# Attention and gated FFN on one core: scores and P V as separate TensorE operations, strided P V in eight array tiles and four PSUM banks, under a new order

## The chip, the cores and the metric

The kernel runs on one core of a Trainium2 chip. The metric is device time in microseconds, from one launch to its end, taken as the median of a few runs. One further run was taken by the hardware profiler; all rows below come from it.

## What is computed

Attention over 8 batches and 8 heads with 576 positions and a head size of 64, then a gated feed-forward network over the 4608 tokens. Half of the heads see the last 32 positions (local), the other half see every 32nd earlier position (strided):

```python
scores = scale * np.matmul(q, k.transpose(0, 1, 3, 2))
rel = pos[:, None] - pos[None, :]
mask_local = (rel >= 0) & (rel < stride)                      # stride = 32, heads 0..3
mask_strided = (rel >= 0) & (pos[None, :] % stride == pos[:, None] % stride)   # heads 4..7
attn = softmax(np.where(masks, scores, -1e9))
x = np.matmul(attn, v)            # regrouped to (4608, 512)
xn = x / rms(x) * rms_g           # then, 512 -> 1536 -> 512:
out = (silu(xn @ w_gate) * (xn @ w_val)) @ w_out
```

## The kernel before

**Two kinds of TensorE work.** The feed-forward part is a long row of large products with a 128x128 weight and 512 columns (lines L579, L655, L1043, L1208, L1431, L1632 of the profile, "GEMM" below). Each takes one weight load and one matmul on the engine. The attention part is many small fp32 products, which take two weight loads and two matmuls each. In the trace one such product is therefore two records of each kind.

**Attention is done in 32 items**, eight batches times four pairs of heads; in each batch the order of pairs is local, strided, local, strided (KCO). For one item there are two bursts of small products and a softmax between them:

- `scores`: local, L290, 36 products (72 records), 64x32 weights against 64 columns; strided, L296, 64 products (128 records), 64x18 weights against 18 columns. They write `pair_`, a PSUM tile of two banks. The strided ones use two row halves of the array and, in each, two of the four 32-column groups: four tiles, all into the first bank.
- `soft`: DVE scales and masks out of `pair_` into a SBUF tile (L324; pp0, pp1, pT0, pT1 by turns), takes the row maximum (L326); ACT does the exponentials, for the odd items with DVE or GpSimd; then a reciprocal, a product and a 32x32 transpose (L344).
- `values` (P V): local, L307, 44 products (88 records), from four row groups into two column halves, eight tiles, in `pair_` and `acc01` (two banks each); strided, L313, 64 products (128 records), from four row groups, each into one column half: four tiles, in the two banks of `acc01`. For items 4 to 7 `acc01` is in use elsewhere and all of P V goes to `pair_`; the local ones are then done in two halves.
- `evac`: ACT or DVE copies the result to `raw` (L378, L380).

**Operations and the order.** Every step is recorded as an operation in `Plan`: an engine, what it reads and writes, and a function that issues all of its instructions in a row. `visit(s, v)` records the scores of item s and the P V of item v; where both are given, they are ONE TensorE operation, so that nothing can stand between them. An operation of strided scores and local P V has 64 + 44 products, one of local scores and strided P V 36 + 64. `Plan.order` then issues the operations in a sequence that the text `ORDER` gives: it is decoded to an index and an engine for each step (some operations may go to one of two or three engines). Within an engine the sequence is that of the program; between engines semaphores hold it. `evac` also reads a key "sv", which `soft` writes: the copies of item v come after the scaling of item s.

**Where the visits lie.** The first five items come at the start, before the FFN has input. Visits then stand beside the GEMMs of the first chunks of 512 tokens, the last of them about 800 us into the span.

Of the kernel before, what the change touches and what calls it, by code (L numbers as in the profile page):

```python
# [23 lines left out]
STRIDE = 32  # L24
NROW = S // STRIDE
P = 128
# [34 lines left out]
    "c-rk*S!^W7d9M1ax~lJcx_j=E91b}om&@g`%O#iGU25+`T4}XfuB6p{!8&3~mSjnmZ3&VsCsve1vaVb(VkEKyBys!@1j%y(1Of7thrH!EK!6x|PIXoHa1G=&Kpt2#=;^"  # L61
    "7h`s+Ww|NH+TgV+lR(mcz4$_z9yY(|I~nBM*7yZXIGg<Dr6i<`cAnZCl#I*ji=%FlA|p=VDLcCXF1?j}^bre89y9@Wp=`UQHCM!UvcoN?b{I}4lR$F|1*wL512?QN~@j"
    "lDUx@*f*BbolR^^H-10td15hSPR+%CS9lcz4P>6NBr<SIW%&nmxljz$lZ1D=m=Q0Gi5IfeqoO-yXn}&fnEE{p56Pi#h>>UetN87uV;t89NK?fokBnUi>&|o$3Gwa-d9<"
    "#{?RYHi@*5rueyFM`{AEgKlrj){bHr@-jAz)_{lQK{%H2g&wqdL*%$3kKbvWP+G~G8I<4RN=%dfR7=Au{|I_N4`SI`maP{Ml8iVYk6aC-((H1d3B$W@|uaMUJt#{s;ef"
    "hgTc=?0uweP?8+Iw%ki{s&KtpbBL>0Z?PZSv~M2iObW`C9nyZ-lGgZoIJahX2&-55~8@cPqa5=FP9)u6`#z|IN2r!5jCd(Q8TcQqXwe`Nr4cllAzS6Y;ZWnwz(t+<Y`V"
    "^~n6g4?p$H!`Tz?#L;x^kw<2arw>K9AB-Mbug~F|H)=O3)$8}wtJmgkUAQ}3xH5Zo{)LOx*4%Sf<Ezc5Mo(TEUCiRObMfk#q<1Sh-F@Ixa(!dxTH0<`Z{B}JUus<&E#G"
    "~2E4wk%x-@rjA!{Y+`R(K%&L-)p&C}JL-S*$_m?v0s)7c~&Q5+pxKN_vA{cP>4uTG>}tDDhEbS%k^CQ-7wn2jn+=`dZKo*z__sFw|g>zypi*1wyrCFxt~a{8^qY4UOU&"
    "2jqjT=wB?_FLHpdoRAQm!=Oy@3fNU+o)0b=Qr!-w`#A~YOltPR~qp*>Swds-(`(Bs6Cfd<CE1ah?B;8Tu<ZYs<moT%fe<FC3i>dt6_Z@*2A#b2^**5@N!hCU5MiF`21a"
    "Nf=*4J9Cemv{NeGof2=iFZ|$yiTER+dx!vlwvSzTB;#!jVHGk1x@aKDDf9{w+yF1$%Me*{sA1qCUgCh$e^{8hr`G?}gcws6T$Nh>sGv#$Wx9|4Oy4~)gxbMvQTUEcYvE"
    "kcO>)f@Yt`|DCbvT$0JUbiN>CjFrJGQJ&5)RsxD2y6mGt}zQVqj*wnV<T}wpH;qy_3f+-|B54({*Q$Hb?9AnZ*^unKlg@W^{cHJ0WM5+iTam?Rwi~&D69jrnQ|~TZzR?"  # L70
    "7P%o433`|<F(+f`b#Ce02-%h3#^uY?%K;yp<7fNa<ELHb?DSgAovkLbs}_4L>zLJSWieUEhRHNDc>g7~8nPqP?C@>Y>a<v^$!5iShK+}FR~Ff&1;)na-1(tCUFq^ZYj+"
    "8w4YE+*T3tO(HfrSP^5Q>|g(b2)PsYRlB-3Py%n>%4BEv4FgEk>&n=Pl=Aiayd?d@KDt4qGDk?OBVW~Ik|MP`%H(tN_n^iqtVKQlfu^NuzgeEV(E@BS2iG9Gk)0{uULU"
    "c1}syy(JutI<ICZ*X&|`L}C_YSoo09yhah8hed}>`$`!S~ge1z3L_0!1eREcP5D|anekW(aL6JZDYu?Z~%Cx;uFZcjguScC|Gx^(=Ylsb;1DoN1j1p!?XM$TA%jN^1$u"
    "eo`amugQ#gYr|mv!7?#yEs$LBxx_&}OQ!!dOiu7fDbzNU<FT488xM^#{8Lc+0O=-kg-PUYur6CHyNLDI_>w+G@5T<*xa1*>fSogr$dh7BkH4M7r;ikKQogJR=wPOMIr&"
    "m4B9H`9)4$#JOgBlctLu@e}v=-?ydio_-3myH*OvjJo$19OR)^6j~isidT;<|{1<8PQ~{@*l~oHIrhj-L4!6b;O92L-JFwTK6GhSJw@CCliX8U7Lv!>Iswr-NyI0DsC|"
    "C*ZiT$5Im+`i8FYKw|=IhfW<HGrq_w+=zf_@prU-#HPS`z3-2G1TGp^oLPvBuw{fsYeukm-EK4;%d@~tjih2=oreL}EbP<3b`8sMES6BZVHk|lCZi71EG8ThhOXg1ZP+"
    "e%sLd>cKltQ>bhJmU7NdhqyGCikVwOgX1uQ<j>x1v~!Lv8FH<8mKCaIbR(WzdKI7ah0o%0e5(G1w&bgZ7`02l+%fkOrm6Q*4XG(zLxG9m;#(>5J249_(Iagm062_M3Yb"
    "82fE<@!`8Zo91GvQBJLy;-a2h@>fj>lA@`k8wBXSFY=q0b?6ulMsdpK4Xzhyb1cohPHW(13e0`N5Fje#xlBf%QWu2apPWo{W`vnqif96G(;J?z>$s4v<W)R`AH6lY3R5"
    "{j~_Qz=?c@AO^VP<9Idb;Li}4ez!(P8X!P7|zz_A%t*JeXTKfIBo*?MioA)6LJ&N!##Mf6jI)|3EBZp6urOF{hA`T;O#v|g$Hf$JJt6P8*q^}YbE?rv2QEw5?>-ai9#r"
    "r#s+q!(E6=AC#te^VUR?x2sBN3#KG+0~%8X<TL`Mx$ndW+igjW%teUJq5TpeshR)<N2(%HeHjWHz->Y>rUJ^IQ>_&~?J*K)=us(hS^xV+!*D>2|v<Cu-x61^9Ul2boTM"  # L80
# [1856 lines left out]
```

## Time and profile before

| | |
|---|---|
| median of 3 runs | 1015.37 us (1014.62 to 1020.02) |
| the profiled execution | 1013.67 us |
| its span, first to last instruction | 1011.9 us |
| TensorE busy (matmul) | 949.3 us, 94% |
| VectorE busy | 747.2 us, 74% |
| ScalarE busy | 429.3 us, 42% |
| GpSimd busy | 231.9 us, 23% |
| mean granted TensorE clock | 0.96 |

TensorE is the engine to read. Its 10,244 matmuls are pipelined and their ends are modelled, so the start of one record against the start of the next tells more than the busy time. An idle time that a row ascribes to "issue" is one for which the profile shows no semaphore that was waited for.

### The profile page before, as it was taken

Reading aid. Unit: us, or ns where it says so; the run is one execution under the profiler, and the core shown is the slowest. Engines: PE = TensorE matmul, PEld = TensorE weight load, DVE = VectorE, ACT = ScalarE, POOL = GpSimd, SP = SyncE. Lnnn points to the kernel's source line nnn. Section 1 sums busy time; section 2 is a strip of 40 time slices with the busy share of each in tenths; the row PEclk is TensorE's granted clock in tenths of the full one; section 3 lists DMA queues with packets and bytes.
Section 4 is the critical chain, followed back from the end, with each engine's and each line's share of the span. In section 5 each row is a group of like instructions: output and inputs, shape, how many; then the busy total and the mean of one; then the engine's idle time right before and its main releaser. Section 6 shows DMA issues by size and latency. Waiting matters only on the chain.

```text
span 1011.9 us, 24518 instructions
## 1 busy us (share of the span) xinstructions
PE 949.3 (94%) x10244; PEld 772.5 (76%) x10244; DVE 747.2 (74%) x1247; ACT 429.3 (42%) x1006; POOL 231.9 (23%) x198
## 2 busy tenths in 40 slices
PE   4799998999989899999899999999998999999998
PEld 2687876778868787778677878887777788888887
DVE  4779987878757889978467888745486898446884
ACT  5678755233224447333443544442233634233240
POOL 2131233024223411122212322200001140003521
PEclk9689999999999999999989999999898999999999
DMA  9736666676564777838645569873354587765552
GB/s 347 307 142 223 215 221 213 236 282 255 166 229 148 249 249 228 307 149 298 248 157 191 188 202 316 303 277 126 125 202 134 165 282 266 275 243 203 177 163 107
DMA packets 95102, 222.97 MB, mean 220 GB/s; under 512 B 9616, under 2 KB 28688, under 8 KB 94992
## 3 DMA queue, kind: packets, MB, share of 16 engines
q1 hardware_dynamic: 94560, 220.85, 62.8%
q8 instruction: 80, 1.31, 0.5%
q10 hardware_dynamic: 432, 0.56, 0.2%
q14 instruction: 30, 0.25, 0.1%
HBM read 174.19 MB, written 47.19 MB: 219 GB/s over the span
## 4 chain that ended last, share of the span: by engine, by line
PE 58%; DMA 3%; DVE 2%; issue 2%; SPq 1%; POOL 0%; ACT 0%; POOLq 0%; DVEq 0%
PE acc L1632 10%; PE g L1632 7%; PE v L1632 7%; PE acc L1431 6%; PE v L1431 4%; PE g L1431 4%; PE g L1043 3%; PE acc L1043 3%; PE v L1043 3%; PE pair L1043 2%; PE g L1208 2%; PE acc L1208 2%; PE v L1208 2%; PE acc L313 2%; DMA xl<-to 1%
## 5 line engine op out<-in xcount | busy, mean ns | idle before, releaser
L579 PE MATMUL g<-xh,wg 128*128 128x512 f32 x184 | 60.1, 409 | 3.5 <-DVE e L594 3.5
L579 PE MATMUL v<-xh,wv 128*128 128x512 f32 x184 | 60.4, 410 | 0.1
L579 PEld LDWEIGHTS g<-xh,wg 128*128 128x128 f32 x184 | 34.7, 195 | 11.7 <-DVE e L594 4.7
L579 PEld LDWEIGHTS v<-xh,wv 128*128 128x128 f32 x184 | 35.5, 197 | 8.2 <-ACT or L1795 0.5
L710 POOL TENSOR_TENSOR tt<-tt 128x256 f32<-128x256 f32 (+1 forms) x29 | 25.1, 872 | 68.4 <-DVE tt L710 25.1
L579 PE MATMUL v<-xl,wv 128*128 128x512 f32 x92 | 37.3, 405 | 0.0
L579 PE MATMUL g<-xl,wg 128*128 128x512 f32 x92 | 36.8, 400 | 0.0
L579 PE MATMUL acc<-xh,wv 128*128 128x512 f32 x104 | 35.6, 426 | 1.1 <-DVE wg L623 1.1
L579 PE MATMUL acc<-xh,wg 128*128 128x512 f32 x104 | 33.8, 407 | 0.0
L1632 PE MATMUL acc<-wg,wv 128*128 128x512 f32 x102 | 31.1, 416 | 0.2 <-DMA wv<-wsv 0.2
L330 ACT ACTIVATE pT<-pT,mx 128x64 f32<-128x64 f32 x80 | 26.7, 335 | 10.2 <-DVE mx L326 10.2
L1632 PE MATMUL acc<-wv,wv 128*128 128x512 f32 x102 | 30.6, 410 | 0.0
L592 ACT ACTIVATE e<-g 128x512 f32<-128x512 f32 x23 | 13.7, 597 | 39.4 <-PE g L579 32.6
L1650 ACT ACTIVATE or<-g 128x512 f32<-128x512 f32 x24 | 14.4, 599 | 37.7 <-PE g L1632 37.4
L342 POOL TENSOR_TENSOR pp<-pp,mx 128x288 f32<-128x288 f32 (+1 forms) x7 | 6.7, 963 | 101.8 <-DVE mx L340 92.9
L655 PE MATMUL acc<-or,hh 128*128 128x512 f32 x96 | 30.1, 394 | 0.0
L296 PEld LDWEIGHTS pair<-xx,xx 64*18 64x18 f32 x2048 | 18.3, 94 | 12.9 <-issue 8.3
L330 ACT ACTIVATE pp<-pp,mx 128x64 f32<-128x64 f32 x80 | 26.7, 339 | 2.7 <-DVE mx L326 2.7
L296 PE MATMUL pair<-xx,xx 64*18 64x18 f32 x2048 | 20.1, 181 | 7.4 <-issue 4.0
L378 ACT COPY raw<-acc 128x256 f32<-128x256 f32 (+7 forms) x41 | 19.0, 538 | 18.1 <-PE acc L313 18.1
L324 DVE SCALAR_TENSOR_TENSOR pT<-pair,cb 128x640 f32<-128x640 f32 (+1 forms) x16 | 10.2, 638 | 21.9 <-PE pair L307 10.8
L579 PEld LDWEIGHTS acc<-xh,wv 128*128 128x128 f32 x104 | 21.4, 208 | 6.3 <-DVE wg L623 1.5
(878 smaller groups left out, 2982.4 us busy)
## 6 DMA issues: line engine op xcount, KB each, us to landing
wv<-wsv SPq DMA_DIRECT2D x36, 512.0 KB, 7.0
wg<-wsg SPq DMA_DIRECT2D x26, 512.0 KB, 7.2
or<-tg SPq DMA_DIRECT2D x22, 512.0 KB, 5.7
th<-tg SPq DMA_DIRECT2D x21, 512.0 KB, 5.6
tl<-tg SPq DMA_DIRECT2D x21, 512.0 KB, 5.7
xx<-in_qT_dram SPq DMA_DIRECT2D x32, 288.0 KB, 5.7
xx<-in_kT_dram SPq DMA_DIRECT2D x31, 288.0 KB, 5.4
vt<-in_vs_dram SPq DMA_DIRECT2D x16, 512.0 KB, 7.2
```

The source lines that it names most:

```text
L296: nc.tensor.matmul(out=pair_[32 * y:32 * y + NROW, 0, NROW * g:NROW * g + NROW], lhsT=q[r, z:z + NROW], rhs=k[r, z:z + NROW], start=True, ...
L313: nc.tensor.matmul(out=dst[0][64 * (y // 2):64 * (y // 2) + 64, y % 2, c], lhsT=v[k, j], rhs=t[k, 32 * j:32 * j + NROW], start=True, stop= ...
L330: nc.scalar.activation(out=tv[:, g], in_=tv[:, g], func=AF.Exp, bias=m[:, g:g + 1], accum_out=z[:, g:g + 1])
L378: nc.scalar.copy(out=d, in_=s)
L579: nc.tensor.matmul(out=out, lhsT=wt[:, w, sl], rhs=xhl[x, kc], start=(n == 0 and i == 0), stop=(n == KC - 1 and i == 2))
L655: nc.tensor.matmul(out=acc[t], lhsT=x[h][:, sl], rhs=wt[:, w], start=(u == 0 and i == 0), stop=(u == NU - 1 and i == 2))
L710: elementwise(width, lambda e: both(e).tensor_tensor(out=dst(), in0=a(), in1=b(), op=ALU.subtract), [], keys)
L1043: nc.tensor.matmul(out=banks[bk], lhsT=w, rhs=X[a, k].tile(y), start=start and k == 0 and i == 0, stop=stop and k == 1 and i == 2, skip_gr ...
L1208: nc.tensor.matmul(out=banks[bks[j]], lhsT=tile(v, k, j), rhs=x.tile(y), start=start and k == 0 and i == 0, stop=stop and k == KT - 1 and ...
L1431: nc.tensor.matmul(out=banks[bks[j]], lhsT=w.tile(v, k, j), rhs=x.tile(k, y), start=start and n == 0 and i == 0, stop=stop and n == KT - 1 ...
L1632: nc.tensor.matmul(out=banks[bk], lhsT=w, rhs=xtile(a, k, y), start=start and k == 0 and i == 0, stop=stop and k == 1 and i == 2, skip_gro ...
L1650: op("ACT", act(CH, True), 0, lambda: nc.scalar.activation(out=temp(dst), in_=banks[bk], func=AF.Copy, scale=scale), reads=bank_keys(bk), ...
```

## The change

- `visit` records the scores and the P V as two operations, each with its own place in the order. The largest has 64 small products. The scores of item s stand ahead of the P V of item v in the list.
- Strided P V: for each of eight j, four row groups times two column halves are issued, so eight tiles follow each other, and each row group has its own PSUM bank, two in `pair_` and two in `acc01`. Items 6 and 7 are done in two halves in `pair_`. The host lays V out to suit (`vs`).
- Strided scores: two row halves times four column groups, eight tiles, into both banks of `pair_`, 18 columns in every 64. Scaling reads them there (`flat`).
- The first memset clears all of `pair_` (1024 columns, before 128).
- `evac` of a strided item copies two pieces per chunk of 512 tokens instead of one, and no longer reads "sv".
- `ORDER` is another text. The number of matmuls of every line is the same.

```diff
-    op("DVE", 200, -1, lambda: nc.vector.memset(pair_[:, :, 256:320], 0.0), writes=PRK)
+    op("DVE", 1100, -1, lambda: nc.vector.memset(flat, 0.0), writes=PRK)
...
-        for g in range(16):
-            for y in range(4):
-                r, z = slice(64 * (y // 2), 64 * (y // 2) + 64), PAD + NROW * (16 * (y % 2) + g)
-                nc.tensor.matmul(out=pair_[32 * y:32 * y + NROW, 0, NROW * g:NROW * g + NROW], lhsT=q[r, z:z + NROW], rhs=k[r, z:z + NROW],
-                                 start=True, stop=True)
+        for j in range(8):
+            for z, y in enumerate(QZ):
+                for h in range(2):
+                    r, a = slice(64 * h, 64 * h + 64), PAD + NROW * (8 * z + j)
+                    nc.tensor.matmul(out=pair_[32 * y:32 * y + NROW, h, 64 * j:64 * j + NROW], lhsT=q[r, a:a + NROW], rhs=k[r, a:a + NROW],
+                                     start=True, stop=True)
...
-        for j in range(16):
-            for y in range(4):
-                k, c = slice(32 * y, 32 * y + NROW), slice(NROW * j, NROW * j + NROW)
-                nc.tensor.matmul(out=dst[0][64 * (y // 2):64 * (y // 2) + 64, y % 2, c], lhsT=v[k, j], rhs=t[k, 32 * j:32 * j + NROW],
-                                 start=True, stop=True)
+        for j in range(8):
+            for z in zs[1:] + zs[:1]:
+                r, c = slice(32 * QZ[z], 32 * QZ[z] + NROW), 320 + NROW * j
+                for h in range(2):
+                    g = 8 * h + j
+                    nc.tensor.matmul(out=dst[z // 2][64 * h:64 * h + 64, z % 2, c:c + NROW], lhsT=v[r, g], rhs=t[r, 32 * g:32 * g + NROW],
+                                     start=True, stop=True)
...
-            pair_[:, 0, 0:G * w].rearrange("q (g k) -> q g k", k=w), tv, mstr)
+            flat.rearrange("q (g k) -> q g k", k=64)[:, :, 0:w], tv, mstr)
...
-                moves.append((o.rearrange("p (i s n) -> p s n i", s=2, n=16),
-                              dst[0][:, :, 0:288].rearrange("p s (n i) -> p s n i", i=NROW)[:, :, :, i0:i1]))
+                    moves.append((o.rearrange("p (i s n) -> p s n i", s=4, n=8)[:, z:z + 2],
+                                  src[:, :, 320:320 + 8 * NROW].rearrange("p s (n i) -> p s n i", i=NROW)[:, :, :, i0:i1]))
...
-        op("ACT", act(t1 - t0, True) + 97 * (len(moves) - 1), 0, fn, reads=keys + ["sv"], writes=[("raw", c % NX, p) for c in cs],
+        op("ACT", act(t1 - t0, True) + 97 * (len(moves) - 1), 0, fn, reads=keys, writes=[("raw", c % NX, p) for c in cs],
...
-            op("PE", cost, 0, lambda fns=tuple(fns): [f() for f in fns], reads=reads + [("tb", v % 4), ("vt", v % 2)],
-               writes=writes + [k for k in keys if k not in writes])
...
+        if s is not None:
+            op("PE", 970 if its[s][1] < 2 else 1070, 0, lambda: scores(s), reads=[("xx", slot_of(s, 0)), ("xx", slot_of(s, 1)), ("xp", slot_of(s, 1))],
+               writes=PRK)
...
+            for dst, zs, keys in ([((pair_, pair_), (0, 1), PRK), ((pair_, pair_), (2, 3), PRK)] if 4 <= v < 8 else
+                                  [((pair_, acc01), (0, 1, 2, 3), PRK + A01K)]):
+                op("PE", (1250 if local else 1150) - 50 * (4 <= v < 8), 0, lambda dst=dst, zs=zs: values(v, dst, zs),
+                   reads=[("tb", v % 4), ("vt", v % 2)], writes=keys)
```

On TensorE, before, at the eighth strided scores of the program (about 293 us into the span). L579 is the FFN's first product; L296 the strided scores, L307 the local P V of the item before; a count behind a row is of products.

```order
L579 MATMUL v<-xh_874,wv_719 128x512 x2
L579 MATMUL v<-xl_883,wv_719 128x512
L296 MATMUL pair<-xx_80,xx_83 18x18 x64
L307 MATMUL pair<-pT_97,vt_85 64x32 x2
L307 MATMUL acc_69<-pT_97,vt_85 64x32 x4
L307 MATMUL pair<-pT_97,vt_85 64x32 x2
L307 MATMUL pair<-pT_97,vt_85 64x64 x2
L307 MATMUL acc_69<-pT_97,vt_85 64x64 x4
```

On TensorE, now, at the same scores (L298 is the old L296, L564 the old L579).

```order
L564 MATMUL acc_71<-xh_897,wv_721 128x512 x2
L564 MATMUL acc_71<-xl_900,wv_721 128x512
L298 MATMUL pair<-xx_80,xx_83 18x18 x64
L564 MATMUL acc_70<-xh_536,wg_1146 128x512 x2
L564 MATMUL acc_70<-xl_538,wg_1146 128x512
L564 MATMUL acc_70<-xh_665,wg_1146 128x512 x2
L564 MATMUL acc_70<-xl_714,wg_1146 128x512
L564 MATMUL g<-xh_897,wg_929 128x512 x2
```

Before, the 108 small products stood in one piece; now 36 GEMM products stand between the scores and the same local P V.

On TensorE, before, at the local scores and the strided P V that come next (L290 and L313).

```order
L579 MATMUL acc_70<-xl_883,wg_903 128x512
L290 MATMUL pair<-xx_82,xx_81 32x64 x36
L313 MATMUL acc_69<-pT_98,vt_86 64x18 x64
L579 MATMUL g<-xh_606,wg_987 128x512 x2
L579 MATMUL g<-xl_616,wg_987 128x512
```

On TensorE, now, the end of a local P V and the start of a strided P V in the middle of the attention (L309 is the old L307, L317 the old L313, L1416 the old L1431).

```order
L309 MATMUL pair<-pT_97,vt_85 64x64 x2
L309 MATMUL pair<-pT_97,vt_85 64x32 x4
L1416 MATMUL acc_71<-wv_3744,or_4227 128x512 x3
L1416 MATMUL acc_71<-wg_3966,wg_3928 128x512 x3
L317 MATMUL pair<-pT_98,vt_86 64x18 x2
L317 MATMUL acc_69<-pT_98,vt_86 64x18 x4
L317 MATMUL pair<-pT_98,vt_86 64x18 x4
```

The strided P V now alternates between `pair` and `acc`, and so needs what the local P V left in both to be copied out; here six GEMM products stand between the two.

## Rows read from the trace of the kernel before

**Rows 1.** The page: busy us of each engine; granted clock in 40 slices, tenths.

```profile
PE 949.3 (94%) x10244; PEld 772.5 (76%) x10244; DVE 747.2 (74%) x1247; ACT 429.3 (42%) x1006; POOL 231.9 (23%) x198
...
PEclk9689999999999999999989999999898999999999
```

**Rows 2.** TensorE's waits, 60 to 812 us: total us, times, longest.

```profile
PE acc L307 <- issue: 7.6, 4, 2.0
PE pair L307 <- issue: 6.2, 2, 4.0
PE acc L313 <- issue: 4.6, 3, 3.9
PE g L1632 <- issue: 4.4, 2, 3.7
...
PE acc L1632 <- issue: 3.1, 1, 3.1
PE pair L290 <- issue: 1.6, 1, 1.6
```

**Rows 3.** DMA queues, whole span, then 295.2 to 299.7 us: packets, MB, share.

```profile
q8 instruction: 80, 1.31, 0.5%
...
q8 instruction: 1, 0.02, 1.3%
```

**Rows 4.** Timeline of TensorE around 296 us: start, length, what, idle before.

```profile
293.78 1.23 PE L296 MATMUL pair<-xx,xx 64*18 64x18 f32 x128
...
299.66 0.38 PE L307 MATMUL pair<-pT,vt 32*64 32x64 f32 x3 [3.99 <-issue]
...
301.57 0.63 PE L579 MATMUL acc<-xl,wv 128*128 128x512 f32 x1
...
302.85 0.63 PE L579 MATMUL acc<-xl,wv 128*128 128x512 f32 x1
```

**Rows 5.** Stages: length, busy us of each engine, granted clock, DMA share, GB/s.

```profile
152.58:156.00 3.42, 3.42 (x16) 2.73 (x9) 0.69 (x1) 2.90 (x4) 0.00 (x0) 0.50 0.50 164
...
790.88:794.29 3.41, 3.41 (x10) 2.66 (x9) 3.38 (x8) 3.27 (x9) 0.00 (x0) 0.50 0.95 253
sum 51.21, PE 47.08 PEld 37.28 DVE 27.89 ACT 14.62 POOL 5.25; mean PE 4.28 PEld 3.39 DVE 2.54 ACT 1.33 POOL 0.48
```

**Rows 6.** Timeline of TensorE, small products without a stall, full clock.

```profile
87.29 0.90 PE L307 MATMUL pair<-pp,vt 32*64 32x32 f32 x48
...
100.19 0.39 PE L579 MATMUL g<-xl,wg 128*128 128x512 f32 x1
...
100.87 0.39 PE L579 MATMUL g<-xl,wg 128*128 128x512 f32 x1
101.19 1.23 PE L296 MATMUL pair<-xx,xx 64*18 64x18 f32 x128
102.34 0.50 PE L655 MATMUL acc<-or,hh 128*128 128x512 f32 x1
...
253.21 0.24 PE L307 MATMUL pair<-pp,vt 32*64 32x32 f32 x2
...
254.07 0.32 PE L307 MATMUL pair<-pp,vt 32*64 32x64 f32 x8
```

**Rows 7.** The same view: local scores and strided P V in one operation.

```profile
390.02 0.97 PE L290 MATMUL pair<-xx,xx 64*32 64x64 f32 x72
390.92 2.06 PE L313 MATMUL acc<-pT,vt 18*64 18x18 f32 x128
392.90 0.50 PE L1431 MATMUL acc<-wv,xl 128*128 128x512 f32 x1
```

**Rows 8.** The copies of P V on ACT: shortest, median, longest in ns.

```profile
L378 ACT COPY raw<-acc x41: 220/405/1150, 32.7 to 806.0; 128x256 f32<-128x256 f32 x14, 128x64 f32<-128x64 f32 x10, 128x128 f32<-128x128 f32 x5, 128x512 f32<-128x512 f32 x4
```

**Rows 9.** Stages as in Rows 5: the attention beside the first chunks.

```profile
60.00:353.00 293.00, 275.79 (x3713) 224.09 (x3712) 237.21 (x401) 139.43 (x349) 88.88 (x78) 0.97 0.63 218
353.00:418.00 65.00, 63.50 (x853) 51.20 (x852) 58.10 (x99) 34.02 (x90) 11.71 (x9) 1.00 0.75 245
```

More of the change, by code (lines that the diff above doesn't have):

```diff
@@ L65 @@
[L65 to L80, printed above, removed]
@@ L104 @@
+    "Pg6xfc2!Krx2vG4WFtdHAf*;2)%(>;z`G_$M3Rn=r&NipmYb5r$;wArD=LZq&G?G$>ymfLipcuRDe!O0eT|J8&(0CBKevv<@^H*U;th2#pDTlld}}J)AKPXZuS0rpZl4"
+    "+qDCzs$K3p1zyAdzrr2)"
 )
@@ L324, in soft @@
         op("DVE", dve(G * w), 0, lambda: nc.vector.scalar_tensor_tensor(out=ov, in0=sv, scalar=0.125, in1=mk, op0=ALU.mult, op1=ALU.add),
-           reads=["cb"] + PRK, writes=[tk, "sv"])
+           reads=["cb"] + PRK, writes=[tk])
         op("DVE", dve(G * w), 0, lambda: nc.vector.tensor_reduce(out=m, in_=tv, axis=AX.X, op=ALU.max, negate=True), reads=[tk], writes=[mk_])
@@ L355, in evac @@
             cs.append(c)
[L356 to L372 removed]
+            for z in zs[::2]:
+                src, o = dst[z // 2], raw[c % NX][:, p, max(0, lo - CH * c):hi - CH * c]
+                if p > 1:
+                    i0, i1 = (lo - base) // STRIDE, (hi - base) // STRIDE
+                    moves.append((o.rearrange("p (i s n) -> p s n i", s=4, n=8)[:, z:z + 2],
+                                  src[:, :, 320:320 + 8 * NROW].rearrange("p s (n i) -> p s n i", i=NROW)[:, :, :, i0:i1]))
+                    continue
+                m = 32 * (QB[z + 1] - QB[z])
+                a, e = max(lo - base, 32 * QB[z]) - 32 * QB[z], min(hi - base, 32 * QB[z + 2]) - 32 * QB[z]
+                at = base + 32 * QB[z] - CH * c
+                if a == 0 and e == 2 * m:
+                    moves.append((raw[c % NX][:, p, at:at + e].rearrange("p (z q) -> p z q", z=2), src[:, :, 320:320 + m]))
+                    continue
+                for f in range(2):
+                    a1, e1 = max(a, m * f), min(e, m * f + m)
+                    if a1 < e1:
+                        moves.append((raw[c % NX][:, p, at + a1:at + e1], src[:, f, 320 + a1 - m * f:320 + e1 - m * f]))
             lo = hi
@@ L416, in visit @@
                 load(s + 2)
-        else:
+        if v is not None:
+            local = its[v][1] < 2
+            for dst, zs, keys in ([((pair_, pair_), (0, 1), PRK), ((pair_, pair_), (2, 3), PRK)] if 4 <= v < 8 else
+                                  [((pair_, acc01), (0, 1, 2, 3), PRK + A01K)]):
+                op("PE", (1250 if local else 1150) - 50 * (4 <= v < 8), 0, lambda dst=dst, zs=zs: values(v, dst, zs),
+                   reads=[("tb", v % 4), ("vt", v % 2)], writes=keys)
+                evac(v, dst, zs, keys)
             done_i.add(v)
```

116 lines of the change are left out of this document (45 added, 71 removed).

## The prediction

> **What bounds the kernel now.** I read the page first: TensorE is busy for 949.3 of 1011.9 us and no other engine passes 74% [rows 1]. So its 62.6 us without work, and whatever makes its work slow, decide. Next I read what ended its idle times. Between 60 and 812 us, where the visits lie beside the GEMMs, the six largest waits on "issue" make 7.6 + 6.2 + 4.6 + 4.4 + 3.1 + 1.6 = 27.5 us [rows 2]; no wait on another engine is among them. Then one of these places, in order of time: strided scores run from 293.78 us, the local P V behind them is cut off, and TensorE stands still for 3.99 us before 299.66 [rows 4]. In that gap the queue of kind "instruction" carries one packet [rows 3].
>
> That row tells what "issue" is. Over the span this queue carries 80 packets, 1.31 MB, so 16.4 KB each [rows 3]. TensorE has 10,244 matmul and 10,244 weight-load records [rows 1]; 20,488 / 80 = 256 per packet. So each packet brings 256 TensorE instructions. GEMM products use two of them per 0.227 us (three products from 100.19 to 100.87 us [rows 6]), a block lasts 29 us, and the next packet has long landed. Small products use two per 8 to 15 ns, and a block is over in 1 to 2 us, before the next has come. An operation with 108 products is 432 instructions and is sure to hold most of a block.
>
> A second loss hangs on the first. The granted clock falls to 0.5 in eleven stretches after 60 us, 51.2 us in all [rows 5], which is 1.2 GHz instead of 2.4. Ten of them begin within some 2 us of a stop of at least 1 us in TensorE's stream; the one of rows 4 is among them. In it three GEMM products take from 301.57 to 302.85 us, 0.427 us each against 0.227.
>
> **The change part by part.** All sums go against the profiled execution, 1013.7 us; the median of the runs, 1015.4, is 1.7 above it.
>
> *Array tiles for strided P V.* 128 records take 2.06 us; less the 0.2 us that a lone record takes (two take 0.24 [rows 6]) and over 127 steps that is 14.6 ns a record [rows 7]. Is this the number of tiles? The local P V in halves, which uses four tiles too, takes (0.90 - 0.2) / 47 = 14.9 ns [rows 6]; the same product in eight tiles goes from 253.21 to the end of its last record at 254.39, (1.18 - 0.2) / 87 = 11.3 ns [rows 6]. So the tiles count. One end is 11.3: same weights, same tiles, but more columns. The other is the 8.1 ns of strided scores, (1.23 - 0.2) / 127 [rows 6]: same 18 columns, narrower weights. I take the middle, 9.7: 127 x 4.9 ns = 0.62 us for each of the 14 items that get eight tiles (items 6 and 7 keep four), **8.7 us less**; ends 5.9 and 11.6.
>
> The Trainium skill speaks against this term: "TensorE: Matmul & The Clock Gate", section "Wait — 56ns, not 53.3ns?", says that start to start never drops below about 25 ns however few the columns, so that tiles would bring nothing here and the sum would be 8.7 us higher. The traced records start 8 to 15 ns apart, so the trace doesn't agree, and the sum goes by the rows.
>
> *Strided scores in eight tiles.* Nothing here has their shape. I keep 8.1 ns; bounds are half of it (8 us less over 16 items of 127 steps), and the 10.8 ns of local scores in eight tiles, (0.97 - 0.2) / 71 [rows 7] (5.5 us more).
>
> *More operations.* 24 bursts stand alone that were parts of one (22 fused visits, two halves). The switch from GEMM to small product costs 101.19 - 100.87 = 0.32 us against 0.227 of a plain step [rows 6], so **2.2 us more**; at most 0.2 each, 5 us.
>
> *Instruction packets.* I cut the order of before and the new one into blocks of 256 TensorE instructions (four per small product, two per GEMM product), at the places where the trace stops. After 60 us, before has 14 blocks with at most 7 GEMM instructions, and 11 with 8 to 30. The new order has 2 and 13, since GEMMs stand between nearly all bursts. Going through the timeline stop by stop, the 14 hold some 22 of the 27.5 us [rows 2], 1.6 each, and the 11 the other 5, 0.5 each. Now: 2 x 1.6 + 13 x 0.5 = 9.7, so **17.8 us less**. If all 15 stop like the first kind, 3.5 less; if the mixed ones never stop, 24 less. In the start, up to 60 us, the bursts stand nearly as before, and the chain through the first softmaxes ends last: 0, within 4 either way.
>
> *Clock.* The slow stretches hold 47.1 us of TensorE work [rows 5]; at the full clock this work needs 0.227 / 0.427 of that, so they cost 22 us. With 9.7 of 27.5 us of stops left I expect 4 of the 11 stretches, so **14 us less**; ends 4 and 20.
>
> *New waits.* Strided P V now writes `pair` too, so it waits until the local P V before it is copied out, and the scores behind it wait until its own copies are done. A copy takes 0.4 us on ACT [rows 8]; strided items need up to four pieces, two more than before, some 11 us more of ACT in all, on an engine with 42% [rows 1]; the GEMMs between hide it. At the tight places (three to nine GEMM products, 0.7 to 2 us, some eight of them) I expect 0.5 us each: **4 us more**. Queued behind a waiting burst are the GEMMs themselves, so such a wait is paid in full. Ends 0 and 15. The wider memset lies before the first scores, which wait for their input anyway: nothing; uncovered, about 1 us. Dropping "sv" lets copies go earlier: nothing, ACT isn't late.
>
> Sum: 1013.7 - 8.7 + 2.2 - 17.8 - 14 + 4 = 979.4, and 1.7 for the median: **981 us**.
>
> **The rivals.** *A, the forecast*, 981, with 959 to 1000 as its own range.
>
> *B, the stops stay.* The blocks with 8 to 30 GEMM instructions stop like the full ones, and each stop brings its slow stretch. Then only tiles, switches and new waits remain: 1015.4 - 8.7 + 2.2 + 4 = 1013. For it: four stops in rows 2 stand at a GEMM line (L1632, 3.7 us the longest), just behind a burst, so a few GEMMs don't always help. Against: the 11 such blocks of before held 0.5 us each.
>
> A page has a rule that also ends here: the Trainium skill, "Runtime: NRT & Kernel Launch", section "Instruction fetch mechanics", says that instructions are fetched in 16 KiB blocks while the current one runs and that crossing a boundary is mostly hidden; then "issue" would be something else and separate operations would give nothing. The trace agrees on the size (16.4 KB), but the 3.99 us in rows 4 are not hidden.
>
> *C, DVE takes part of it back.* From 60 to 353 us DVE is busy for 237 of 293 us, and in the next stage for 58.1 of 65, 89% [rows 9]. Of the gain some 20 us fall into the first stage; 237 / 273 is 87%. If chains through DVE then give back half of the 34 us, the time is 998. Against: in rows 2 no DVE wait is among the six largest.
>
> *D, slower: the hand-over of `pair` and `acc01` bounds each visit.* Every burst needs what the last one left to be read or copied. If each of some 30 hand-overs from P V to the next burst waits for four copies and two switches between engines, 4 x 0.4 + 0.3 = 1.9 us, that is 57 us against a gain of 38 without the 4: 1015 - 38 + 57 = 1034. It decides from about 1.3 us per hand-over. Against: at most places 12 or more GEMM products (2.7 us) stand between.
>
> That the change doesn't do what it says is ruled out by the order: GEMMs do stand there.
>
> **How the numbers follow.** A 0.72, B 0.09, C 0.13, D 0.06; the likeliest gives 981. The range, 959 to 1004, holds most of A and of C and leaves out B and D and A's low tail (faster scores, no stops left). The bound of 0.5% is what a measurement of this kernel can tell from no change. Faster: A and nearly all of C, 0.84. Same: B, 0.09. Slower: D and a bit of C, 0.07.
>
> **What would show it.** Each strided P V record of eight tiles 8 to 11 ns behind the last, a burst of about 1.4 us instead of 2.06. "Issue" in TensorE's waits after 60 us down from 27.5 to about 10. Stretches at 0.5 from 51 to about 19 us. Waits of TensorE on ACT or DVE copies (`raw`) up by a few us, not tens. The forecast is wrong if "issue" stays above 20 us, if the clock stays low without stops, or if waits on `raw` or on DVE's softmax steps come to 15 us or more.

## The result and the profile after

The changed kernel takes 972.8 us, the median of four runs (970.6 to 981.0), against 1015.2 us: a ratio of 0.960, 95% interval 0.953 to 0.967. The forecast was 981 us, with 959 to 1004. The profiled execution took 974.5 us (span 972.6), which is 39.2 us less than the 1013.7 of the kernel before.

A correction ahead of the reading: front part and prediction call the strided items that keep two halves "6 and 7". Items 4 to 7 all have their P V in `pair`; the strided ones among them are 5 and 7. The count of 14 with eight tiles is right.

The page of the changed kernel, busy us by engine and the granted clock, answers [rows 1]:

```profile
PE 928.7 (95%) x10244; PEld 753.5 (77%) x10244; DVE 758.5 (78%) x1266; ACT 412.1 (42%) x1001; POOL 252.1 (26%) x216
...
PEclk6589998999999999999999999999999999999999
```

TensorE has 20.6 us less busy time and 18.7 us less idle time in the span. What ended the idle time is in TensorE's waits, 60 to 780 us (total us, times, longest), beside [rows 2]. L298 is the strided scores, L317 the strided P V, L291 the local scores:

```profile
PE pair L298 <- issue: 7.9, 2, 4.5
PE acc L317 <- issue: 4.5, 2, 2.3
PE g L564 <- DVE e L579: 2.2, 1, 2.2
PE acc L1617 <- issue: 1.0, 1, 1.0
PE pair L291 <- issue: 0.9, 2, 0.7
PE pair L317 <- issue: 0.9, 1, 0.9
...
PE pair L317 <- ACT wv L1328: 0.5, 1, 0.5
PE pair L317 <- DVE pT L348: 0.5, 1, 0.5
```

"Issue" is 7.9 + 4.5 + 1.0 + 0.9 + 0.9 = 15.2 us where all such rows of before came to 28.8. The longest wait on DVE is that of a GEMM on `e`, which was there before with 3.2 us. No row names `raw`, the copies of P V: the new use of `pair` by strided P V costs next to nothing.

The stretches at the lower clock after 60 us (length, busy us of each engine, granted clock, DMA share, GB/s) answer [rows 5], with their last line of sums:

```profile
159.13:162.54 3.41, 3.09 (x29) 2.47 (x30) 2.64 (x4) 0.20 (x2) 1.79 (x3) 0.50 0.95 282
...
619.93:623.34 3.41, 3.41 (x10) 2.64 (x8) 0.69 (x1) 1.08 (x2) 1.87 (x2) 0.50 0.00 0
...
sum 20.46, PE 19.86 PEld 15.59 DVE 9.71 ACT 8.08 POOL 4.58; mean PE 3.31 PEld 2.60 DVE 1.62 ACT 1.35 POOL 0.76
```

Six stretches and 20.5 us, where eleven made 51.2. The one at 619.93 follows the stop that the timeline shows (start, length, what, idle time before it):

```profile
613.98 1.05 PE L298 MATMUL pair<-xx,xx 64*18 64x18 f32 x106
618.45 0.29 PE L298 MATMUL pair<-xx,xx 64*18 64x18 f32 x22 [3.42 <-issue]
```

One burst of 128 records of strided scores is cut after 106 of them, in the middle of one operation that waits for nothing. Count all TensorE records in order of time: weight loads, matmuls and the semaphore instructions between them. For all but about 1 of the 15.2 us of "issue", the first matmul after the gap then stands at position 193 or 194 modulo 256, as it does after the stops of before.

Strided P V, on the same view: the first and the last row of one burst, and the GEMM behind it.

```profile
197.99 0.23 PE L317 MATMUL pair<-pp,vt 18*64 18x18 f32 x2
...
199.20 0.22 PE L317 MATMUL pair<-pp,vt 18*64 18x18 f32 x2
199.35 0.73 PE L564 MATMUL v<-xh,wv 128*128 128x512 f32 x2
```

From 197.99 to the last record's start at 199.22 are 1.23 us for 127 steps, 9.7 ns each, where [rows 7] gave 14.6. The Trainium skill, "TensorE: Matmul & The Clock Gate", section "Wait — 56ns, not 53.3ns?", puts about 25 ns below every such step; this trace does not agree, nor did that of before (14.6).

DVE, in the stages of [rows 9], cut where the same work lies now:

```profile
60.00:335.00 275.00, 266.61 (x3616) 214.58 (x3616) 239.90 (x413) 127.03 (x318) 82.57 (x71) 0.99 0.65 226
335.00:400.00 65.00, 62.22 (x1052) 50.39 (x1051) 56.30 (x91) 31.30 (x90) 24.64 (x19) 0.97 0.82 271
```

The first stage is 18 us shorter with the same DVE work, 87% instead of 81% busy, and TensorE's waits on DVE did not grow (6.8 to 4.3 us). Rival C would have shown here.

**The sum of the profiled pair.** Stops 28.8 to 15.2, 13.6 us less. Lower clock: TensorE work in it 47.1 to 19.9 us, and at full clock this takes 0.227 / 0.427 of the time [rows 4, 6], 12.7 less. Tiles 14 x 0.62 = 8.7 less. Waits on DVE, ACT and DMA 8.8 to 5.0, 3.8 less. Switches about 2 more. Together 36.8 of 39.2 us.

### The profile page after: what moved, and what is told of

The parts are those of the page before. It is cut to its first block, busy times and chain, and to the rows that moved or that the text cites. A ratio compares the mean times of both kernels' runs of the same rounds, so it can differ in the third digit from the quotient of the medians.

```text
span 972.6 us, 24559 instructions
## 1 busy us (share of the span) xinstructions
PE 928.7 (95%) x10244; PEld 753.5 (77%) x10244; DVE 758.5 (78%) x1266; ACT 412.1 (42%) x1001; POOL 252.1 (26%) x216
## 4 chain that ended last, share of the span: by engine, by line
PE 87%; DVE 6%; issue 3%; ACT 1%; DMA 1%; SPq 0%; DVEq 0%; ACTq 0%
PE acc L1617 9%; PE acc L564 8%; PE acc L1416 7%; PE g L564 7%; PE g L1617 6%; PE v L1617 6%; PE v L564 6%; PE v L1416 5%; PE g L1416 5%; PE v L1028 3%; PE acc L1028 3%; PE g L1028 3%; PE acc L640 3%; PE pair L298 2%; PE g L1193 2%
## 5 line engine op out<-in xcount | busy, mean ns | idle before, releaser
L564 PE MATMUL g<-xh,wg 128*128 128x512 f32 x184 | 61.0, 414 | 2.2 <-DVE e L579 2.2
L564 PE MATMUL v<-xh,wv 128*128 128x512 f32 x184 | 58.4, 398 | 0.0
L564 PEld LDWEIGHTS g<-xh,wg 128*128 128x128 f32 x184 | 36.3, 201 | 10.3 <-DVE e L579 2.6
L564 PEld LDWEIGHTS v<-xh,wv 128*128 128x128 f32 x184 | 33.5, 188 | 6.7
L564 PE MATMUL g<-xl,wg 128*128 128x512 f32 x92 | 37.5, 408 | 0.0
L382 ACT COPY raw<-pair 128x128 f32<-128x128 f32 (+7 forms) x59 | 18.7, 363 | 42.7 <-PE pair L317 18.8
L564 PE MATMUL acc<-xh,wv 128*128 128x512 f32 x104 | 33.6, 403 | 2.4 <-DVE xh L531 1.5
L564 PE MATMUL v<-xl,wv 128*128 128x512 f32 x92 | 35.9, 390 | 0.0
L564 PE MATMUL acc<-xh,wg 128*128 128x512 f32 x104 | 34.4, 413 | 0.0
L298 PEld LDWEIGHTS pair<-xx,xx 64*18 64x18 f32 x2048 | 18.1, 95 | 20.6 <-issue 15.6
L298 PE MATMUL pair<-xx,xx 64*18 64x18 f32 x2048 | 20.2, 183 | 14.5 <-issue 11.4
L695 POOL TENSOR_TENSOR tt<-tt 128x256 f32<-128x256 f32 (+1 forms) x27 | 23.0, 854 | 40.9 <-DVE tt L695 21.8
L1617 PE MATMUL acc<-wg,wv 128*128 128x512 f32 x102 | 28.9, 392 | 0.0
L564 PEld LDWEIGHTS acc<-xh,wv 128*128 128x128 f32 x104 | 19.9, 192 | 7.2 <-ACT or L1765 1.6
L507 DVE RECIPROCAL srt<-srt 128x128 f32<-128x128 f32 x28 | 25.0, 921 | 0.2 <-ACT srt L504 0.2
L564 PEld LDWEIGHTS acc<-xh,wg 128*128 128x128 f32 x104 | 19.9, 197 | 4.8 <-DVE hl L579 0.4
```

What stands on the lines that cost most here:

```text
L298: nc.tensor.matmul(out=pair_[32 * y:32 * y + NROW, h, 64 * j:64 * j + NROW], lhsT=q[r, a:a + NROW], rhs=k[r, a:a + NROW], start=True, stop ...
L382: nc.scalar.copy(out=d, in_=s)
L507: op("DVE", 890, at, lambda q=q: nc.vector.reciprocal(out=roots["srt"][:, q:q + P], in_=roots["srt"][:, q:q + P]), writes=["srt"])
L564: nc.tensor.matmul(out=out, lhsT=wt[:, w, sl], rhs=xhl[x, kc], start=(n == 0 and i == 0), stop=(n == KC - 1 and i == 2))
L695: elementwise(width, lambda e: both(e).tensor_tensor(out=dst(), in0=a(), in1=b(), op=ALU.subtract), [], keys)
L1617: nc.tensor.matmul(out=banks[bk], lhsT=w, rhs=xtile(a, k, y), start=start and k == 0 and i == 0, stop=stop and k == 1 and i == 2, skip_gro ...
```

## The experiments

**Theory.** TensorE's stream comes in packets of 256 instructions; where a packet is run through before the next has landed, TensorE stops, and the clock falls behind it. Most of the gain is fewer such places, the rest eight tiles. **Rivals:** the gain is the new order on all engines and "issue" belongs to the bursts; or P V is faster by its banks, not by its tiles.

All ratios are to the kernel before, on the same chip and in the same group of runs. Behind the first measurement (rows one and two) there are three groups: `c_again`, `a_shift16`, `a_shift52`, `a_refused` (median of before 1011.7 us); `a_4tiles`, `b_8tiles`, `b_shift18`, `b_shift38` (1008.2); `b_split`, `b_split8`, `a_shift64` (1010.5). "Stops" are all "issue" rows of TensorE's waits after 60 us, "low clock" the stretches at 0.5 that begin after 60 us, without one at the very end. Both are of one profiled execution, which in `a_shift64` is 6 us faster and in `b_shift18` 5 us slower than the median:

| run | us | ratio [95%] | stops | low clock | waits on DVE / ACT / DMA |
|---|---|---|---|---|---|
| before | 1015.2 | 1 | 28.8 | 51.2 | 6.8 / 0 / 2.0 |
| changed | 972.8 | 0.960 [0.953, 0.967] | 15.2 | 20.5 | 4.3 / 0.7 / 0 |
| c_again | 972.9 | 0.960 [0.956, 0.965] | 11.9 | 27.3 | 4.7 / 0.7 / 0 |
| a_shift16 | 956.6 | 0.945 [0.941, 0.948] | 1.8 | 10.2 | 4.6 / 0.7 / 0 |
| a_shift52 | 983.8 | 0.972 [0.968, 0.977] | 17.0 | 30.7 | 4.1 / 0.7 / 1.0 |
| a_shift64 | 978.1 | 0.969 [0.966, 0.973] | 9.1 | 17.0 | 4.1 / 0.7 / 0.3 |
| a_refused | 1021.3 | 1.010 [1.007, 1.014] | 21.3 | 61.4 | 23.9 / 4.5 / 0.5 |
| a_4tiles | 979.3 | 0.970 [0.967, 0.973] | 8.8 | 27.3 | 4.8 / 0.7 / 0 |
| b_shift18 | 1019.2 | 1.010 [1.007, 1.014] | 36.5 | 64.9 | 6.0 / 0 / 3.5 |
| b_shift38 | 1050.3 | 1.041 [1.037, 1.044] | 50.0 | 85.4 | 4.9 / 0.2 / 1.0 |
| b_split | 990.6 | 0.981 [0.978, 0.985] | 3.9 | 23.9 | 4.9 / 0.9 / 13.8 |
| b_8tiles | 1008.4 | 0.999 [0.996, 1.002] | 33.2 | 47.8 | 4.1 / 1.0 / 1.8 |
| b_split8 | 992.7 | 0.984 [0.981, 0.987] | 7.6 | 27.3 | 7.5 / 2.3 / 13.5 |

### Moving the boundaries and nothing else

A few tiny products go ahead of the first warm-up product. Each is four TensorE instructions, so 16 of them move every later boundary between packets by 64 instructions. The edit (n is 16, 52 or 64 in the changed kernel, 18 or 38 in the one before):

```diff
+    def warm(n):
+        for _ in range(n):
+            nc.tensor.matmul(out=bank["v"][0:32, 0:4], lhsT=ebuf[0:32, 0:32], rhs=ebuf[0:32, 0:4], start=True, stop=True)
+        nc.tensor.matmul(out=bank["v"], lhsT=ones, rhs=ebuf, start=True, stop=True)
-    for _ in range(2):
-        op("PE", 1700, -1, lambda: nc.tensor.matmul(out=bank["v"], lhsT=ones, rhs=ebuf, start=True, stop=True), reads=["ones", "wz"], writes=["v"])
+    for n in (16, 0):
+        op("PE", 1700, -1, lambda n=n: warm(n), reads=["ones", "wz"], writes=["v"])
```

**The changed kernel again.** 

> The changed kernel once more, with nothing edited, beside which the three others of this group are read on the same chip. All theories: 0.96 of the kernel before (0.953 to 0.967), TensorE stops ascribed to issue after 60 us about 15 us, time at the lower clock after 60 us about 20 us.

Measured: 0.960, stops 11.9, low clock 27.3 us. The ratio is that of the first measurement. The stops are not all the same ones: this execution stopped for 1.0, 0.8 and 0.6 us before 296.7, 726.8 and 769.1 us, where the first did not, and not for the 1.0 us before 494 us, where the first did. The longest stop of the first, 4.51 us, has nearly gone, at the same record of the same burst (timeline; first the first execution, then this one):

```profile
153.90 1.04 PE L298 MATMUL pair<-xx,xx 64*18 64x18 f32 x106
159.45 0.32 PE L298 MATMUL pair<-xx,xx 64*18 64x18 f32 x22 [4.51 <-issue]
```

```profile
156.40 0.29 PE L298 MATMUL pair<-xx,xx 64*18 64x18 f32 x22 [0.24 <-issue]
```

The transfer on the instruction queue that lies before this record began 4.7 us after the packet's first record in the first execution and 1.4 us after it here. So the order sets where a stop can be, and does not by itself set how long it is.

**16 tiny products.** 

> Edit: 16 tiny extra products (64 TensorE instructions) at the very start, under the wait for the first data. They do nothing but move every later boundary between two packets of 256 TensorE instructions by 64 instructions; order, tiles, banks and every wait of the kernel stay. Theory (a packet that is run through before the next one has landed stops TensorE): laid over the starts of the changed kernel's trace, the moved boundaries leave fewer packets that are filled with small products, and stops of 10 to 12 us instead of 15 after 60 us; with the clock that they cost, 3 to 7 us faster than the changed kernel. Rival (the stops belong to the bursts, to the semaphores at their heads or to the order, not to the count of instructions): stops at the same places, 15 us, time within 2 us of the changed kernel.

Measured: 0.945, 16.3 us faster than the changed kernel beside it, and 55 us faster than before. The theory had the sign and the rival is out, but the effect is over twice what I expected: nearly all stops went. TensorE's waits of this run, 60 to 765 us (lines are four higher, L302 the strided scores), and the burst that was cut at 613.98 above:

```profile
PE g L568 <- DVE e L583: 2.9, 1, 2.9
PE pair L295 <- issue: 0.9, 1, 0.9
PE pair L302 <- issue: 0.5, 1, 0.5
...
PE pair L321 <- issue: 0.4, 1, 0.4
```

```profile
601.27 1.23 PE L302 MATMUL pair<-xx,xx 64*18 64x18 f32 x128
```

The same 128 records run through in one piece, with the same work and order around them. The low clock is down to two stretches, from 148.5 and from 162.1 us. At the second stands the GEMM's wait of 2.9 us on DVE. Ahead of the first, TensorE waited no longer than 0.5 us, between bursts of small products, so not every low stretch needs a stop; all those that came with stops are gone.

**52 tiny products.** 

> Edit: as the run with 16 tiny products, with 52 of them (208 instructions), the worst place for the boundaries by the same reckoning. Theory (packets): 18 to 22 us of stops instead of 15 after 60 us, and 3 to 9 us slower than the changed kernel. Rival (bursts or order): stops at the same places, time within 2 us of the changed kernel.

Measured: 0.972, 10.9 us slower than the changed kernel, above the 3 to 9; stops 17.0 us, a little under the range, low clock 30.7. Set record against record, this trace is 4.6 us behind `c_again` at the first strided scores. That is what the 52 products themselves take, which I had put at nothing. At 34 us it is only 0.2 us behind, because the stops in the start are shorter here (1.5 and 1.9 us against 3.6, 1.7 and 2.3). A stop of 3.6 us before 51.4 us makes it 3.4 us at 60 us, and the rest, up to 11.0 us at the end, comes later, at cut bursts.

**64 tiny products.** 

> Edit: the changed kernel with 64 tiny extra products (256 TensorE instructions) at the very start: as much extra work and more than in the runs with 16 and 52, but the boundaries between packets fall at the same instructions as without them. Theory (only the place of the boundaries counts): stops at the same places and of 11 to 16 us after 60 us, ratio 0.955 to 0.965. Rival (the extra products act at the start, by the clock or the loads, and not by the boundaries): as with 16 or with 52, 0.945 or 0.972.

Measured: 0.969, above the theory's range, with 9.1 us of stops, below it. By the trace the products themselves take 5.5 us up to the first strided scores (14.08 against 8.54 us), and it is 6.3 us behind `c_again` at 60 us: the boundaries lie where they did, and nothing is given back in the start. From there to the end it gains 7.3 us on `c_again`. Its stops are at places where one or the other execution of the changed kernel stopped, but the burst that was cut at 613.98 above, and in `c_again` too, ran through here. Less the 6.3 us the ratio is 0.963, inside the range. So the rival is half right: products that leave the boundaries in place cost some 6 us in the start. With 16 of them the trace is 1.0 us behind at the first strided scores, 0.8 us ahead at 60 us and 18.6 us ahead at the end, and that gain the boundaries make.

**The kernel before, 38 tiny products.** 

> Edit: the kernel before with 38 tiny extra products (152 TensorE instructions) at the very start, which do nothing but move the boundaries between packets of 256 instructions to the worst place by the trace of before: 21 packets instead of 14 are filled with small products alone. Theory (packets): stops after 60 us 34 to 40 us instead of 29, 8 to 16 us slower than before with the clock that they cost. Rival (stops belong to the joint operations as such, wherever the boundaries lie): stops of 29 us, time within 3 us of before.

Measured: 1.041, 42 us slower where 8 to 16 were expected, with no other change than where the boundaries lie. Stops rise from 28.8 to 50.0, more than the 34 to 40 expected, and low clock from 51 to 85 us. TensorE's waits, 60 to 840 us (L317 is the strided P V, L311 the local one):

```profile
PE acc L317 <- issue: 17.2, 8, 4.5
PE pair L311 <- issue: 14.2, 5, 4.1
PE acc L311 <- issue: 12.3, 3, 4.7
```

Sixteen stops in three rows. In the profiled pair: stops +21.2, the clock some +15 (0.468 of the work in 34 us more), the start +4.0 by 66 us (1.4 at the first strided scores), other waits -2.7; together 37.5 of a difference of 34.6 us.

**The kernel before, 18 tiny products.** 

> Edit: as the run with 38 tiny products, with 18 of them (72 instructions), the best place for the kernel before: 12 packets filled with small products alone instead of 14. Theory (packets): stops after 60 us 22 to 27 us instead of 29, 2 to 8 us faster than before, and still over 25 us behind the changed kernel with its 16 tiny products, since the joint operations leave no place for the boundaries that is free of them. Rival (stops belong to the joint operations): 29 us and the time of before within 3 us.

Measured: 1.010, 11 us slower, where the theory had it faster and the rival within 3 us. The stops grew to 36.5 us, the long ones all at a boundary, so they are of the same kind. What failed is the reckoning: two packets fewer are filled with small products, but the cut ones stopped longer (5.2 us before 504.2 us, 5.0 before 723.7). The count of such packets alone does not give the sum; how long a packet is under way counts as much, and that I can't compute from the order. So the theory tells where stops lie, and its sums of them failed here and in the run with 38.

### Together or apart

**Put together again, in the new order.** For nine items the large products between scores and strided P V go ahead of the scores:

```diff
+            for i in seq[a + 1:b]:
+                if self.ops[i][1] & later:
+                    later.add(i)
+                else:
+                    early.append(i)
...
+            seq[a:b + 1] = early + [sc, pv] + [i for i in seq[a + 1:b] if i in later]
```

> Edit: in the new order, for nine items the strided P V is put directly behind the local scores that it followed in the kernel before; the large products that stood between go ahead of the scores. Tiles, banks and all other operations stay. Theory (packets): packets filled with small products alone rise from 3 to 8 of 80, stops after 60 us from 15 to 20 to 25 us, stretches at the lower clock by three to five (10 to 17 us more at half speed, 5 to 8 us of time): 8 to 16 us slower than the changed kernel. Rival (the gain of the order is elsewhere, in waits on other engines; the separate operations bring nothing of their own): within 3 us of the changed kernel, with stops of 15 us.

Measured: 1.010; 48 us slower than the changed kernel, and slower than before. Neither theory had this size. Stops are 21.3 us, as the theory said. But TensorE's waits, 60 to 830 us (L344 strided P V, L325 strided scores, L593 and L1646 GEMMs), also hold this:

```profile
PE acc L344 <- issue: 8.6, 4, 3.3
PE pair L344 <- issue: 5.5, 3, 2.0
PE acc L593 <- DVE hl L608: 5.2, 1, 5.2
PE pair L325 <- issue: 4.9, 2, 3.2
PE pair L325 <- DVE raw L411: 3.7, 2, 2.7
PE g L593 <- DVE e L608: 3.0, 1, 3.0
PE v L1646 <- ACT tt L1664: 2.8, 1, 2.8
```

Waits on DVE and ACT rise from 5.4 to 28.4 us. Here the scores come later, by 12 to 120 GEMM products (120 x 0.227 = 27 us), and with them the softmax on DVE, which was 87% busy. In the profiled pair: stops +9.4, other waits +23.5, clock +15 (0.468 of the work in 34 us more): 48 of 49. So separate operations are worth a second thing, which neither theory named: the scores may run far ahead of the P V that they used to share an operation with. How much of the 23.5 us a new order of the other engines would take back is not shown, since they keep the order made for the early scores.

**Taken apart, in the old order.** In the kernel before, the scores of each joint operation go ahead of the large products that stood before them:

```diff
+                first, second, deps = self.joint[i]
+                at, ns = len(out), 0
+                while ns < AHEAD and at and out[at - 1][0] not in deps and out[at - 1][0] not in self.joint:
+                    at -= 1
...
+                out.insert(at, (i, "PE", first))
+                out.append((i, "PE", second))
```

> Edit: the kernel before with its tiles and its order on all engines, but each joint TensorE operation taken apart: its scores go ahead of (mostly) 24 of the large products that stood before them, so that 24 large products lie between scores and P V. Theory (packets: of 80, those filled with small products alone fall from 15 to 4): stops after 60 us from 29 to 10 to 18 us, the time at the lower clock from 52 to 20 to 35 us, 18 to 34 us faster than before (ratio 0.966 to 0.982). Rival (the gain of the change is its new order on all engines; taking the operations apart brings nothing by itself, or the scores that come earlier upset VectorE): ratio 0.99 or more.

Measured: 0.981, 20 us faster than before, the low end of the range. It has none of the new order, none of the new tiles. Stops fell to 3.9 us, below the range, and the low clock to 23.9. A new wait took part of it back, by TensorE's waits from 60 to 800 us (L313 is the strided scores):

```profile
PE pair L313 <- DMA xx<-in_kT_dram: 5.8, 2, 3.5
PE g L599 <- DVE e L614: 3.7, 3, 3.1
PE pair L313 <- DMA xx<-in_qT_dram: 3.4, 2, 2.3
PE pair L313 <- issue: 1.7, 1, 1.7
```

The scores now stand ahead of their loads; waits on DMA rise from 2.0 to 13.8 us. In the profiled pair: stops -24.9, clock -12, DMA +11.8, DVE and ACT -1.0: 26 us less, of which 21.4 were measured. The other 5 us I can't place.

### Tiles or banks

**Four tiles in the new kernel.** The column half becomes the outermost loop, and in the scores (not shown) the row half; banks, data and order stay:

```diff
-        for j in range(8):
-            for z in zs[1:] + zs[:1]:
-                r, c = slice(32 * QZ[z], 32 * QZ[z] + NROW), 320 + NROW * j
-                for h in range(2):
+        for h in range(2):
+            for j in range(8):
+                for z in zs[1:] + zs[:1]:
+                    r, c = slice(32 * QZ[z], 32 * QZ[z] + NROW), 320 + NROW * j
```

> Edit: the changed kernel, with the column half as the outermost loop of strided P V and of strided scores, so that only four array tiles follow each other in either; the same products, banks, data and order of operations. Theory (for P V the tiles in a row set the pace; for scores they do not): strided P V back from 1.23 to 1.85 us for 128 records, strided scores unchanged at 1.05 us, 14 x 0.6 = 8.7 us more work, of which stops take back up to 4 us: 4 to 9 us slower than the changed kernel (ratio to before 0.964 to 0.969). Rival (the four banks made it faster): P V stays at 1.23 us, ratio 0.960.

Measured: 0.970 against 0.960. The burst at 199 us takes 1.71 us for 127 steps, 13.5 ns, a bit less than the 14.6 of before. A half item, which this loop order leaves with two tiles in a row, beside the same half in the changed kernel, four tiles (timeline; first the changed kernel, then this one):

```profile
110.03 1.12 PE L317 MATMUL pair<-pp,vt 18*64 18x18 f32 x64
```

```profile
111.88 1.84 PE L317 MATMUL pair<-pp,vt 18*64 18x18 f32 x64
...
206.08 1.23 PE L298 MATMUL pair<-xx,xx 64*18 64x18 f32 x128
```

Less the 0.2 us of a lone record, 63 steps take 14.6 ns in four tiles and 26 ns in two. So the pace goes with the tiles that follow each other, at equal banks: 26, 14, 9.7 ns for two, four, eight. The work is 14 x 0.48 + 4 x 0.72 = 9.6 us more. By the ratios the time is 10 us more, just above the range, but the two ratios are from different groups; in plain medians it is 6.4 us. In the profiled executions it is 7.9 us more than `c_again`, and there stops take 3.1 us back. Scores, in four tiles again, take 1.23 us as with eight: their 8.3 ns don't hang on it.

**Eight tiles in the old kernel.** The loops of the change, in the joint operations of before:

```diff
+            for j in range(8):
+                for z in zs[1:] + zs[:1]:
+                    r, c = slice(32 * QZ[z], 32 * QZ[z] + NROW), 320 + NROW * j
+                    for h in range(2):
+                        g = 8 * h + j
+                        nc.tensor.matmul(out=dst[z // 2][64 * h:64 * h + 64, z % 2, c:c + NROW], lhsT=v[r, g], rhs=t[r, 32 * g:32 * g + NROW],
+                                         start=True, stop=True)
```

> Edit: the kernel before, with its order and its joint operations, but the 14 undivided strided P V (all but items 5 and 7) in eight array tiles and four PSUM banks, as the change has them, and the strided scores in eight tiles and two banks. Scaling a strided item then takes two DVE instructions in place of one, and a strided copy two pieces per chunk. Theory (tiles make the P V records faster, and nothing else of the change is in this kernel): 128 records of strided P V in 1.25 us instead of 1.85 us, 14 x 0.6 = 8.4 us less work; but packets of 256 instructions are run through sooner, so that stops of 29 us after 60 us stay or grow to 34, and the clock stays: 2 to 9 us faster than before. Rival (the burst was held by its banks or its reads, not by its tiles in a row): P V stays at 1.85 us, time within 2 us of before.

Measured: 0.999 [0.996, 1.002], so no gain beyond 4 us. The records are as fast as in the changed kernel, 1.23 us for 127 steps, so the rival's reason is wrong and its time is right. Stops rose from 28.8 to 33.2 us: where the next packet has not landed, a shorter burst only waits longer. That accounts for about half of the 8.7 us, and where the other half went is not shown.

**Eight tiles, taken apart, in the old order.** 

> Edit: the same taking apart of the joint operations, on the kernel before with strided P V in eight tiles (which by itself gave 0.999). Theory (the eight tiles brought nothing there because a shorter burst waited longer for its packet; where packets are mixed with large products their 8.7 us show): 5 to 9 us faster than the kernel that is only taken apart, ratio 0.957 to 0.976. Rival (the tiles' gain was lost to something else, the second scaling instruction or the second copy): within 2 us of the kernel that is only taken apart.

Measured: 0.984 against 0.981, again no gain; the rival's time. Against `b_split` this profile has 3.7 us more of stops, 2.6 more of waits on DVE and 1.4 on ACT, and 3.4 us more at the low clock: 9 us given for the 8.7. Two of its scores also stand 12 and 3 products later than in `b_split`. The joint operation was not what ate the tiles' gain, as I had thought. In neither variant of the old order did the gain show; in the new order taking it away costs 6 to 10 us. What in the order decides that is open.

## Why the prediction was right

The forecast (981) is 8 us above the measurement. Against its 979.4 for the profiled execution, 974.5 is 4.9 us less: new waits came 7.8 us better, packets and clock 5.5 us worse, and 2.4 us are not placed. The other 3.4 us are the median, put at 1.7 us above the profiled execution and measured 1.7 below. So the mechanism holds, and that the sum comes this close is in part luck, since its errors cancel. By its steps:

- *Tiles*, -8.7: the record step came out at the 9.7 ns that was taken, and where the tiles were taken back in the new kernel it cost 6 to 10 us. But this is no term that stands alone: in the old order the runs show no gain. The forecast had it as one, and that the new order could use it was not foreseen.
- *Strided scores in eight tiles*, 0: right, 8.3 ns before and after, and in four tiles of the new layout.
- *Switches*, +2.2: lone bursts cost 0.99 (local scores), 1.25, 1.21 (local P V) and 1.46 us between GEMMs, some 0.2 us above the step times their records; inside a joint operation the change of burst cost 0.15. About 2 us.
- *Packets*, -17.8: 13.6 in the first profile, 16.9 in `c_again`. The mechanism was right, and the runs that moved the boundaries alone show it as cause, from 1.8 to 17 us in one order and from 29 to 50 in the other. Mis-sized was the count times a mean, which gave 9.7 us. In the first profile one of the two packets that are filled with small products stopped for 4.5 us (0.2 in `c_again`). The 13 mixed ones stopped for 7.1 us (8.3 in `c_again`), so 0.5 each on the mean, but single ones for 0 to 3.6 us. And the 3.4 us before 618.45 stand behind a packet with 43 GEMM instructions, of a kind that the count had left out. `b_shift18` missed by the same reckoning. The page cited there, the Trainium skill's "Runtime: NRT & Kernel Launch", section "Instruction fetch mechanics", has crossings mostly hidden; over all traces here that is so for long packets, and not for short ones (below).
- *Clock*, -14: 12.7 by the same ratio, 20.5 us left where 19 were expected, six stretches where four were. Moving the boundaries moved the low clock with the stops, from 10 to 31 us in the changed kernel and from 51 to 85 in the one before. But stops are not its only company: `b_split` has 3.9 us of them, 13.8 us of waits on DMA and 23.9 us at the low clock.
- *New waits*, +4: not there. After 60 us the waits on other engines fell by 3.8 us, and none is on `raw`. TensorE waited for a copy of P V on ACT twice, 0.5 us each, both before 60 us. `a_refused` shows why the order matters here: where scores no longer lead, 23.5 us of such waits appear.
- *Rivals*: B (stops stay) needed 28 us of "issue". D needed hand-overs of 1.3 us or more, and the only two are the 0.5 us above; its 0.3 us for two switches between engines stands in no row, and in the trace of before a record on DVE or ACT mostly starts 0.04 us after the TensorE record that releases it. C needed waits on DVE, which fell. The argument against C misread its view: one wait on DVE was among the six largest, the fifth in size.

```profile
PE g L579 <- DVE e L594: 3.5, 2, 3.2
```

How the gain of 39 us divides between taking apart and the new order is settled only roughly: taking apart in the old order gave 20 us, after some 12 us were lost again to loads that the old order has too late.

## What to carry over

Count the instructions of an engine in packets before believing a burst's length: a stop in the middle of an operation that waits for nothing, always at the same position modulo 256, is a packet that has not landed, and large products strewn between small ones make it rarer and shorter. Try a few dummy instructions at the start: 16 tiny products were worth 16 us here, the fastest kernel of this study, and 42 us were lost in another by an edit that only shifts the stream, so a difference of 1 to 4% between two versions may be nothing but that. The count of filled packets did not say beforehand which shift would gain: it erred in sign once. A faster burst is worth what the work behind it can take up; price it in the order in which it will run.

## What the runs showed of the hardware

**When a packet is late.** From the records of all thirteen traces, after 60 us: for each packet of 256 TensorE records, the time from its first to its last start, and whether a gap of over 0.8 us follows before the next packet's first record.

| run through in | packets | gap over 0.8 us | mean gap, us |
|---|---|---|---|
| under 1.5 us | 42 | 35 | 2.6 |
| 1.5 to 2.5 | 39 | 23 | 1.7 |
| 2.5 to 3.5 | 41 | 15 | 0.9 |
| 3.5 to 5 | 74 | 23 | 0.6 |
| 5 to 7 | 136 | 8 | 0.2 |
| over 7 | 617 | 1 | 0.1 |

In the 105 gaps of over 0.8 us the next record starts 1.2 to 1.5 us (5th to 95th percentile) after the end of the transfer on the instruction queue. The transfer itself takes about 1.0 us. When TensorE crosses a boundary, the next transfer mostly begins soon after, and later when the queue that carries the data is busy: 1.0 us after the boundary in the median when that queue keeps the DMA engines under 30% busy in the microsecond behind it, 2.8 us when over 90%. This is an association in the traces; no run took the data transfers away. An estimate from these three: some 3.2 to 3.5 us from one boundary to the next packet's first record with a quiet data queue, and 5.0 to 5.3 with a busy one. It fits the table, where stops are rare from 5 us on.

**Tiles and pace.** Strided P V needs 26, 13.5 to 14.6 and 9.7 ns a record with two, four and eight tiles in a row; strided scores, with weights of 18 columns, 8.3 ns with four as with eight. What holds the last two is open.

**The start.** 16, 52 and 64 tiny products (64, 208 and 256 instructions) delayed the first local scores by 1.8, 5.6 and 6.9 us. They delayed the first strided scores, which had waited 2.2 us for a load without them, by 1.0, 4.6 and 5.5 us.
